# Attention rows to columns by DMA transposes, casting loads of v, and loads ordered a tile sooner, in an attention and gated-MLP kernel

## The chip, the cores and the metric

One core of one Trainium2 chip. The metric is the device time of one execution in microseconds, the slowest core's; here there is one core. Every ratio below is the mean time of one kernel's fast runs over the mean time of the other's fast runs in the same rounds, with a 95% interval, so it is not quite the ratio of the medians that stand beside it.

## The reference

```python
# q, k, v: 8 batches x 8 heads x 576 positions x 64, float32
scores = q @ k.T / 8                      # heads 0-3: window of the last 32 positions
attn   = softmax(where(mask, scores, -1e9))   # heads 4-7: every 4th of the last 128 positions
x      = (attn @ v).transpose(0, 2, 1, 3).reshape(4608, 512)
h      = x @ w_in                         # 512 -> 2048
out    = (h * sigmoid(beta * h)) @ w_out  # 2048 -> 512, float32
```

The scores are small (q and k are 0.1 times a normal draw), so the softmax is nearly flat inside its window.

## The kernel before

Everything is bfloat16 on TensorE. The 4608 tokens are cut into 9 tiles of 512. For each tile, 16 slots of w_in (four matmuls of 512 columns each, then tanh on ScalarE and a gate on VectorE) and 4 output blocks of w_out (16 matmuls each) run. Between them, in the same stream, the attention of a later batch is computed: scores S, exponentials, a multiplication by a mask, value matmuls V, and a division by the row sums ("norm"), which gives rows. The w_in matmuls need columns (`xT`), so TensorE transposes the rows:

```python
for name in [n for n in names if n[0] == "X"]:
    ...
    def back(e, x=x, j=j, g=g, n=n, m=m):
        xp = bank(g, BF16)
        for a in range(m):                      # m = 3 (96 columns each) or 4 (72 each)
            nc.tensor.transpose(xp[:, a * n:(a + 1) * n], xs[x, j][:, a]..., ident_b[0:n, 0:n])
    ...
    xcopy[b, x, j] = plan.op([act(S // 2), dve(S // 2)], put, [xop], ...)   # PSUM -> xT
```

For batches 3 to 7, q and k are cast by GpSimd's DMA into rows in DRAM (`s`), and SyncE's DMA transposes bring them into `dk`, `dq` and `raw`; engines then spread them into `qzd`, `kz` and `qd`. v is loaded in 32 bits by SyncE and cast by GpSimd when it is spread:

```python
cs = [cast(b, z, gop[b - 2, 4] + behind, b - 2 + .01 * z) for z in range(2)]
for n, (z, h0) in enumerate(((0, 4), (1, 4), (0, 0), (1, 0))):
    ...
    ld[b]["x", z, h0] = crossbar(b, z, h0, [cs[z]] + war(*key) + extra, b - 2 + .3 + .01 * n)
ld[b]["vp"], ld[b]["vd"] = load_v(b, (gop[b - 2, 6] + ..., gop[b - 2, 6] + ...), b - 2 + .35)
```

The important thing to know about `plan.op(engines, function, deps, priority)` is what it is not. It is a list scheduler that runs while the program is built. It places each operation with estimated durations and so fixes *the order* of the instructions on every engine. On the chip each engine walks down its list and waits only where data or a buffer demands it: in after, GpSimd stood 13.4 us before a spread, and casts behind that spread in its list went out at 190.0 us; put before it in f1, they went out at 168.8.

The softmax here doesn't subtract the row's maximum and nothing guards it: scores larger than these inputs give would overflow.

Of the kernel before, what the change touches and what calls it, by code (L numbers as in the profile page):

```python
# [33 lines left out]
class Plan:  # L34
# [3 lines left out]
    CAPS = {"h": 3, "o": 2, "a": 8}  # L38
# [11 lines left out]
    def run(self, filler=None, filler_until=0.0):  # L50
# [33 lines left out]
        while n_left:  # L84
# [41 lines left out]
            if o.dma:  # L126
                dma_free = max(dma_free, s + d + 900) + o.dma
                o.end = dma_free + 1100
                lanes[e].append(o.end)
# [25 lines left out]
def kernel(  # L155
# [32 lines left out]
    ADDED = 2  # L188

# [15 lines left out]
    def copy(e, out, in_):  # L205
# [23 lines left out]
    xs = {(x, j): const([QT if x < 2 else HT, 3 if x < 2 else C, 2, D], BF16, f"xs{x}{j}")  # L229
          for x in range(4) for j in range(2)}  # L230
# [3 lines left out]
    vd_st = st[0][:].bitcast(FP32).rearrange("p (f h T d) -> p f h T d", f=2, h=4, T=C)  # L234
    vp_st = st[1][:, 0:NI * 4 * D * 2].bitcast(FP32).rearrange("p (c d) -> p c d", d=D)
# [4 lines left out]
        "p (f h T d) -> p f h T d", f=2, h=4, T=C)  # L240
    kT = [const([P, WIN + S], BF16, f"kT{x}") for x in range(2)]
# [99 lines left out]
    def load(queue, args, deps, vt, kb, rate=.4, issue=750):  # L341
        return plan.op(
            [(queue, issue)],
            lambda e: dma(queue, *args), deps, vt, dma=kb * 1024 / rate / 1000)
# [15 lines left out]
    def direct_vd(b, deps, vt):  # L360
        rows = v[b, 4:8].rearrange("h (t T) d -> t h (T d)", T=C)
        dst = vd16.rearrange("p f h T d -> p f h (T d)")
        return [load("POOL", (dst[0:80, 0], rows[0:80]), deps, vt, 320, .35),
                load("POOL", (dst[:, 1], rows[16:CT]), deps, vt, 512, .35)]

    def load_v(b, deps, vt):
        rows = v[b, 4:8].rearrange("h (t T) d -> t h (T d)", T=C)
        dst = vd_st.rearrange("p f h T d -> p f h (T d)")
        d = [load("SP", (dst[0:80, 0], rows[0:80]), deps[0], vt, 320, .35),
             load("SP", (dst[:, 1], rows[16:CT]), deps[0], vt, 512, .35)]  # L370
        p = [load("SP", (vp_st, plain_v(b, 0, 0)), deps[1], vt + .001, 768, .2, 3500)]
        return p, d
# [39 lines left out]
    xcopy = {}  # L412

    def attention(b, ld, names, vts):
# [94 lines left out]
        if b < DIRECT:  # L509
            vdeps["P"] = ld["vp"] + [(fill3, fill4)[b % 2]]  # L510
            ops = []
            for f, n in ((0, 80), (1, P)):
                def spread(e, f=f, n=n):
                    copy(e, vd[kv][0:n, f, :, :, 0:D], vd16[0:n, f])
                o = plan.op([("POOL", 1050), ("DVE", 700)], spread, [ld["vd"][f], (fill3, fill4)[b % 2]] + war(("vd", kv)), vt)
                used("vd16", o)
                ops.append(o)
            wrote(("vd", kv))
            vdeps["D"] = ops
        else:  # L520
            def spread(e):
                copy(e, vp[kv][:, :, 0:D], vp_st)
            o = plan.op([("POOL", 1480), ("DVE", 1700)], spread, ld["vp"] + war(("vp", kv)), vt)
            used(("st", 1), o)
            vdeps["P"] = [o]
            ops = []
            for f, n in ((0, 80), (1, P)):
                def spread(e, f=f, n=n):
                    copy(e, vd[kv][0:n, f, :, :, 0:D], vd_st[0:n, f])
                o = plan.op([("POOL", 1050), ("DVE", 1200)], spread, [ld["vd"][f]] + war(("vd", kv)), vt)  # L530
                used(("st", 0), o)
                ops.append(o)
            wrote(("vd", kv), ("vp", kv))
            vdeps["D"] = ops
# [112 lines left out]
        for name in [n for n in names if n[0] == "X"]:  # L647
# [66 lines left out]
    def block_cols(t, tb, vts, lo, hi, cuts):  # L714
        g = Group("o")
# [68 lines left out]
    def loads(b):  # L784
        if b < DIRECT:
            base = -.9
            for n, (z, h0) in enumerate(((0, 4), (1, 4), (0, 0), (1, 0))):
                ld[b]["qk", z, h0] = direct_qk(b, z, h0, war(("st", z)), base + .01 * n)
            wrote(("st", 0), ("st", 1))
            ld[b]["vd"] = direct_vd(b, war("vd16"), base + .05)  # L790
            wrote("vd16")
            ld[b]["vp"] = direct_vp(b, [fill4], base + .06)
        else:
            behind = [ld[b - 1]["x", z, h0] for z in range(2) for h0 in (0, 4)] if b > DIRECT else []
            cs = [cast(b, z, gop[b - 2, 4] + behind, b - 2 + .01 * z) for z in range(2)]
            for n, (z, h0) in enumerate(((0, 4), (1, 4), (0, 0), (1, 0))):
                key = (("dk", b % 2, 0), ("dk", b % 2, 1)) if (z, h0) == (0, 4) else ("dq",) if h0 else (("raw", z),)
                extra = war("vd16") if not h0 else []
                ld[b]["x", z, h0] = crossbar(b, z, h0, [cs[z]] + war(*key) + extra, b - 2 + .3 + .01 * n)
                wrote(*key)  # L800
            ld[b]["vp"], ld[b]["vd"] = load_v(b, (gop[b - 2, 6] + war(("st", 0)), gop[b - 2, 6] + war(("st", 1))), b - 2 + .35)
            wrote(("st", 0), ("st", 1))
# [59 lines left out]
```

## Time and profile before

| | before |
|---|---|
| median of 3 runs | 327.26 us (327.01 to 327.35) |
| span of the profiled run | 325.7 us |
| TensorE busy | 310.3 us, 95% |
| granted TensorE clock | 0.988 |
| TensorE: sum of all matmuls at columns/2.4 + 2.5 ns | 300.6 us |
| TensorE: time between starts beyond that sum | 20.0 us, of it 16.8 before 70 us |

The last two rows are worked out from the trace: the start of each weight load against the start of the one before it, less the pitch of the matmul between them. The pitch is a fit to this trace, in which neighbouring matmuls from 120 to 300 us start 216 ns apart at 512 columns, 42 at 96, 32 at 72 and 29 at 65, in the median. "Wait" below means this excess. It adds up: 1.1 us to the first matmul, 300.6, 20.0, and 4.0 for the last output to leave, 325.7.

Two further views of before: the first is TensorE's line and the clock's in the page's 40 slices (8.1 us each, in tenths); the second is from the list of DMA issues (what, issuing queue, count, KB, median us from issue to landing).

```profile
PE   5878999999999999999999999999999999999995
PEclk9699999999999999999999999999999999999999
```

```profile
st<-in_v_dram SPq DMA_DIRECT2D x5, 768.0 KB, 8.6
...
raw<-s SPq DMA_TRANSPOSE x10, 4.0
...
dk<-s SPq DMA_TRANSPOSE x5, 9.8
dq<-s SPq DMA_TRANSPOSE x5, 4.1
```

Slices are counted from 0: a 9 from slice 4 on is a stream without a hole. v and the transposes of q and k share SyncE's queue, and dk, the first behind v, pays for it: its issue alone holds SyncE for 5.8 to 7.9 us, that of dq for 1.2 to 1.5.

### The profile page before, as it was taken

The page shows a single profiled execution, that of the slowest core. Times are in us where ns is not written, and L with a number is a line of the kernel's source. Part 1 is how long each engine was busy: PE and PEld are TensorE (multiplying, and loading weights), DVE is VectorE, ACT ScalarE, POOL GpSimd, SP SyncE. Part 2 cuts the span into 40 slices and gives each one's busy share as a digit, 9 for nine tenths or more (in the row PEclk, how much of TensorE's full clock was granted, in tenths as well). Part 3 has the DMA queues.
Part 4 walks back from the last instruction along what each step waited for, and adds up shares of the span by engine and source line. Part 5 has one row for each costly group of instructions (what it writes and reads, how often), then busy time and mean ns, then how long its engine had stood idle before and what let it go on. Part 6 is the DMA issues. An engine that isn't in the chain of part 4 may idle for free.

```text
span 325.7 us, 6483 instructions
## 1 busy us (share of the span) xinstructions
PE 310.3 (95%) x2433; PEld 176.2 (54%) x2473; DVE 222.9 (68%) x508; ACT 189.1 (58%) x364; POOL 114.6 (35%) x150
## 2 busy tenths in 40 slices
PE   5878999999999999999999999999999999999995
PEld 3766777655555545555555455545554444444453
DVE  5578777688888879887889868976885443344300
ACT  3577778577757646565746574657464544445411
POOL 7999742602863448335505520551000000000000
PEclk9699999999999999999999999999999999999999
DMA  6999999769805892699689558940000010000121
GB/s 88 173 209 208 204 163 179 142 157 223 146 0 114 235 189 86 129 225 178 166 207 178 135 112 199 190 126 32 34 32 34 32 64 33 34 32 32 45 86 64
DMA packets 69759, 40.04 MB, mean 123 GB/s; under 512 B 50832, under 2 KB 64416, under 8 KB 69408
## 3 DMA queue, kind: packets, MB, share of 16 engines
q0 software_dynamic: 20784, 16.09, 34.8%
q1 hardware_dynamic: 48800, 23.48, 31.2%
q8 instruction: 19, 0.31, 0.4%
q14 instruction: 12, 0.10, 0.1%
q10 hardware_dynamic: 144, 0.07, 0.1%
HBM read 40.37 MB, written 15.34 MB: 171 GB/s over the span
## 4 chain that ended last, share of the span: by engine, by line
PE 85%; DVE 6%; ACT 3%; issue 2%; DMA 2%; POOL 0%; ACTq 0%; DVEq 0%; POOLq 0%
PE bank L720 36%; PE bank L688 35%; PE bank L629 4%; PE bank L656 3%; PE bank L558 2%; DMA st<-in_q_dram 2%; PE bank L398 2%; PE bank L569 2%; DVE g L700 2%; DVE xs L642 2%; ACT tnh L695 1%; PE bank L552 1%; DVE qzd L206 1%; DVE kz L206 1%; PE bank L563 1%
## 5 line engine op out<-in xcount | busy, mean ns | idle before, releaser
L695 ACT ACTIVATE tnh<-bank,beta_half 128x512 bf16<-128x512 f32 (+2 forms) x160 | 102.6, 645 | 89.9 <-PE bank L688 81.5
L688 PE MATMUL bank<-xT,w_in_bf 128*128 128x512 bf16 (+2 forms) x622 | 144.6, 357 | 2.3 <-ACT pt L596 0.5
L720 PE MATMUL bank<-w_out_bf,g 128*128 128x512 bf16 (+1 forms) x570 | 142.0, 373 | 1.3 <-ACT osb L737 0.3
L700 DVE SCALAR_TENSOR_TENSOR g<-tnh,bank 128x512 bf16<-128x512 bf16 (+2 forms) x160 | 100.2, 631 | 59.4 <-ACT tnh L695 57.9
L688 PEld LDWEIGHTS <-w_in_bf 128*128 128x128 bf16 x640 | 58.3, 97 | 49.3 <-issue 3.2
L720 PEld LDWEIGHTS <-g 128*128 128x128 bf16 x592 | 53.8, 98 | 49.8 <-issue 0.5
L596 ACT ACTIVATE pt<-bank 128x288 bf16<-128x288 f32 (+1 forms) x112 | 45.1, 446 | 4.6 <-PE bank L558 2.1
L642 DVE TENSOR_TENSOR xs<-bank,rcp 72x256 bf16<-72x256 f32 (+1 forms) x96 | 44.6, 465 | 3.3
L609 POOL TENSOR_TENSOR pt<-pt,mask_d 128x288 bf16<-128x288 bf16 x22 | 17.3, 800 | 64.8 <-ACT pt L596 62.0
L629 PEld LDWEIGHTS <-pt 128*128 128x128 bf16 x448 | 22.8, 97 | 12.9 <-issue 0.6
L737 ACT ACTIVATE osb<-bank 128x512 f32<-128x512 f32 (+1 forms) x33 | 19.4, 587 | 17.8 <-PE bank L720 16.7
L656 PEld LDWEIGHTS <-xs 72*128 72x128 bf16 (+1 forms) x224 | 15.1, 97 | 13.1 <-DVE xs L642 1.7
L656 PE MATMUL bank<-ident_b,xs 72*128 72x72 bf16 (+1 forms) x224 | 18.6, 200 | 1.4 <-DVE xs L642 1.1
L206 ACT COPY xT<-bank 128x288 bf16<-128x288 bf16 x34 | 13.4, 398 | 9.9 <-PE bank L656 8.6
L206 DVE COPY xT<-bank 128x288 bf16<-128x288 bf16 x30 | 13.1, 436 | 8.0 <-PE bank L656 7.6
L641 DVE RECIPROCAL rcp<-bank 72x4 f32<-72x4 f32 (+1 forms) x96 | 16.7, 174 | 1.7 <-PE bank L629 1.5
L558 PE MATMUL bank<-qzd,dk 128*128 128x144 bf16 x128 | 17.6, 234 | 0.2
L629 PE MATMUL bank<-vd,pt 128*128 128x65 bf16 x256 | 16.5, 193 | 0.5 <-DVE xs L642 0.3
L558 PEld LDWEIGHTS <-dk 128*128 128x128 bf16 x128 | 11.4, 102 | 6.5 <-issue 0.8
L206 POOL CAST vd<-st 80x1024 bf16<-80x1024 f32 (+1 forms) x10 | 10.4, 1053 | 8.2 <-DMA st<-in_v_dram 8.2
L739 DVE TENSOR_SCALAR osb<-bank 128x512 f32<-128x512 f32 (+2 forms) x5 | 2.8, 552 | 13.7 <-PE bank L720 11.6
L609 DVE TENSOR_TENSOR pt<-pt,mask_d 128x288 bf16<-128x288 bf16 x26 | 10.2, 419 | 1.3 <-ACT pt L596 1.2
(107 smaller groups left out, 236.6 us busy)
## 6 DMA issues: line engine op xcount, KB each, us to landing
out_dram<-osb SPq DMA_DIRECT2D x35, 256.0 KB, 2.0
st<-in_v_dram SPq DMA_DIRECT2D x5, 768.0 KB, 8.6
s<-in_k_dram POOLq DMA_DIRECT2D x5, 576.0 KB, 5.7
s<-in_q_dram POOLq DMA_DIRECT2D x5, 576.0 KB, 8.4
st<-in_v_dram SPq DMA_DIRECT2D x5, 512.0 KB, 5.0
w_out_bf<-in_moe_w_out_dram POOLq DMA_DIRECT2D x2, 1024.0 KB, 21.8
st<-in_k_dram POOLq DMA_DIRECT2D x6, 288.0 KB, 9.0
st<-in_q_dram POOLq DMA_DIRECT2D x6, 288.0 KB, 10.2
```

The costliest lines, as they stand in the source:

```text
L206: (nc.scalar.copy if e == "ACT" else E[e].tensor_copy)(out=out, in_=in_)
L558: nc.tensor.matmul(sc[:, a, 0:2 * n], lhsT=dk[kv][:, rp, h4, hf * (CT - P):hf * (CT - P) + P], rhs=qzd[kv][:, :, rp, h4, hf * HT:(hf + 1) ...
L596: nc.scalar.activation(out=pt_of(x, j, n).rearrange("p (a b) n -> p a b n", a=2), in_=sc[:, :, 0:2 * n].rearrange("p a (b n) -> p a b n", ...
L609: E[e].tensor_tensor(out=w, in0=w, in1=m, op=ALU.mult)
L629: nc.tensor.matmul(pv[:, a, h2, :], lhsT=pt[x][:, c], rhs=rhs, start=True, stop=True)
L642: nc.vector.tensor_tensor(out=xs[x, jx][:, a0:a0 + m], in0=pv[0:n, :, :, 0:D], in1=rc[0:n, 0:m].unsqueeze(3).to_broadcast([n, m, 2, D]), o ...
L656: nc.tensor.transpose(xp[:, a * n:(a + 1) * n], xs[x, j][:, a].rearrange("p h d -> p (h d)"), ident_b[0:n, 0:n])
L688: nc.tensor.matmul(bank(g)[:, 0:n], lhsT=w_in_bf[:, kt, fb * P:(fb + 1) * P], rhs=xT[:, kt, xo:xo + n], start=(kt == 0), stop=(kt == NKT - 1))
L695: nc.scalar.activation(out=th[:, 0:n], in_=bank(g)[:, 0:n], func=ACT.Tanh, scale=beta_half[:, fb:fb + 1])
L700: nc.vector.scalar_tensor_tensor(out=g_t[t % 2][:, fb, c0:c0 + n], in0=th[:, 0:n], scalar=1.0, in1=bank(g)[:, 0:n], op0=ALU.add, op1=ALU.mult)
L720: nc.tensor.matmul(bank(g)[:, lo:hi], lhsT=g_t[t % 2][:, fb, tb * P:(tb + 1) * P], rhs=w_out_bf[:, fb, lo:hi], start=(fb == 0), stop=(fb = ...
L737: nc.scalar.mul(out=ob[:, cols], in_=bank(g)[:, cols], mul=0.5)
```

## The change

The intent: take 140 of the 224 transposes of rows off TensorE, which sets the end, and give DMA and the two queues more time by ordering the loads a tile sooner. Cut to its core:

```diff
-    CAPS = {"h": 3, "o": 2, "a": 8}
+    CAPS = {"h": 3, "o": 2, "z": 4, "a": 8}
...
-        g = Group("o")
+        g = Group("z" if t == NTT - 1 else "o")          # last tile: four banks
...
+    def back_dma(b, j, vt_of, vdone):                    # batches 3 to 7
+        rows = dram_pool.tile([S // 2, HD], BF16, name=f"x{b}_{j}")
+        # ... two stores of the plain heads' rows, one of the dilated heads' rows ...
+        cols = xT[:, :, b * S + j * S // 2:b * S + (j + 1) * S // 2]
+        o = plan.op([("SP", 1300)], lambda e: nc.sync.dma_start_transpose(out=cols, in_=rows[:]),
+                    out + [dil], ..., dma=1500, lat=2000)
...
-            ld[b]["vp"], ld[b]["vd"] = load_v(b, (gop[b - 2, 6] + ..., gop[b - 2, 6] + ...), b - 2 + .35)
+            ld[b]["vd"] = direct_vd(b, gop[b - 2, 0] + war(*key), b - 2 + .35)     # GpSimd's DMA, casting
+            ld[b]["vp"] = direct_vp(b, gop[b - 2, 0] + war(("vp", b % 2)), b - 2 + .36)
...
-            cs = [cast(b, z, gop[b - 2, 4] + behind, b - 2 + .01 * z) for z in range(2)]
+            cs = [cast(b, z, gop[b - 3, 12] + behind, b - 2.3 + .01 * z) for z in range(2)]
...
-                ld[b]["x", z, h0] = crossbar(b, z, h0, [cs[z]] + war(*key) + extra, b - 2 + .3 + .01 * n)
+                ld[b]["x", z, h0] = crossbar(b, z, h0, [cs[z]] + war(*key) + extra, b - 2 + .01 * n)
```

More of the change, by code (lines that the diff above doesn't have):

```diff
@@ L127, in run @@
                 dma_free = max(dma_free, s + d + 900) + o.dma
-                o.end = dma_free + 1100
+                o.end = dma_free + (o.lat or 1100)
                 lanes[e].append(o.end)
@@ L188 @@
     ADDED = 2
+    BY_DMA = 3
     pool = lambda name, bufs: ctx.enter_context(tc.tile_pool(name=name, bufs=bufs))
@@ L228 @@
     pt = [const([P, NG[x], P], BF16, f"pt{x}") for x in range(4)]
-    xs = {(x, j): const([QT if x < 2 else HT, 3 if x < 2 else C, 2, D], BF16, f"xs{x}{j}")
-          for x in range(4) for j in range(2)}
+    xsp = [const([QT, 3, 2, 2, D], BF16, f"xsp{j}") for j in range(2)]
+    xsd = [const([HT, C, 2, 2, D], BF16, f"xsd{j}") for j in range(2)]
+    xs = {(x, j): (xsp if x < 2 else xsd)[j][:, :, x % 2] for x in range(4) for j in range(2)}
     st = [const([P, 8 * 512], BF16, f"st{i}") for i in range(2)]
     ks, qs = (s[0:RT].rearrange("p (h e) -> p h e", h=H) for s in st)
-    vd_st = st[0][:].bitcast(FP32).rearrange("p (f h T d) -> p f h T d", f=2, h=4, T=C)
-    vp_st = st[1][:, 0:NI * 4 * D * 2].bitcast(FP32).rearrange("p (c d) -> p c d", d=D)
     rl = xT[0:RT, :, 6 * S:6 * S + R * P].rearrange(
@@ L240 @@
         "p (f h T d) -> p f h T d", f=2, h=4, T=C)
+    vd16_of = [vd16] * DIRECT + [st[b % 2][:, 0:2048].rearrange(
+        "p (f h T d) -> p f h T d", f=2, h=4, T=C) for b in range(DIRECT, B)]
     kT = [const([P, WIN + S], BF16, f"kT{x}") for x in range(2)]
@@ L361, in direct_vd @@
         rows = v[b, 4:8].rearrange("h (t T) d -> t h (T d)", T=C)
-        dst = vd16.rearrange("p f h T d -> p f h (T d)")
+        dst = vd16_of[b].rearrange("p f h T d -> p f h (T d)")
         return [load("POOL", (dst[0:80, 0], rows[0:80]), deps, vt, 320, .35),
                 load("POOL", (dst[:, 1], rows[16:CT]), deps, vt, 512, .35)]
-    def load_v(b, deps, vt):
-        rows = v[b, 4:8].rearrange("h (t T) d -> t h (T d)", T=C)
-        dst = vd_st.rearrange("p f h T d -> p f h (T d)")
-        d = [load("SP", (dst[0:80, 0], rows[0:80]), deps[0], vt, 320, .35),
-             load("SP", (dst[:, 1], rows[16:CT]), deps[0], vt, 512, .35)]
-        p = [load("SP", (vp_st, plain_v(b, 0, 0)), deps[1], vt + .001, 768, .2, 3500)]
-        return p, d
     scratch = {}
@@ L412 @@
     xcopy = {}
+    def back_dma(b, j, vt_of, vdone):
+        rows = dram_pool.tile([S // 2, HD], BF16, name=f"x{b}_{j}")
+        plain = rows[:, 0:HD // 2].rearrange("(i m e) c -> e m i c", e=2, m=QT // 2)
+        out = []
+        for e_ in range(2):
+            out.append(plan.op(
+                [("SP", 500)], lambda e, e_=e_: nc.sync.dma_start(
+                    out=plain[e_], in_=xsp[j][e_ * QT // 2:(e_ + 1) * QT // 2].rearrange("p a x h d -> p a (x h d)")),
+                [vdone[0, j], vdone[1, j]], vt_of[f"X1{j}"], dma=600, lat=2000))
+        dil = plan.op(
+            [("SP", 500)], lambda e: nc.sync.dma_start(
+                out=rows[:, HD // 2:].rearrange("(t r) c -> t r c", r=C),
+                in_=xsd[j][:].rearrange("p r x h d -> p r (x h d)")),
+            [vdone[x, jj] for x in (2, 3) for jj in (2 * j, 2 * j + 1)], vt_of[f"X3{j}"], dma=1100, lat=2000)
+        for x in range(4):
+            wrote(("xs", x, j))
+            for o in out if x < 2 else [dil]:
+                used(("xs", x, j), o)
+        cols = xT[:, :, b * S + j * S // 2:b * S + (j + 1) * S // 2]
+        o = plan.op([("SP", 1300)], lambda e: nc.sync.dma_start_transpose(out=cols, in_=rows[:]), out + [dil],
+                    max(vt_of[f"X1{j}"], vt_of[f"X3{j}"]), dma=1500, lat=2000)
+        for x in range(4):
+            xcopy[b, x, j] = o
     def attention(b, ld, names, vts):
@@ L508, in attention, with spread @@
         vt = vt_of["zVAL"]
-        if b < DIRECT:
-            vdeps["P"] = ld["vp"] + [(fill3, fill4)[b % 2]]
-            ops = []
-            for f, n in ((0, 80), (1, P)):
-                def spread(e, f=f, n=n):
-                    copy(e, vd[kv][0:n, f, :, :, 0:D], vd16[0:n, f])
-                o = plan.op([("POOL", 1050), ("DVE", 700)], spread, [ld["vd"][f], (fill3, fill4)[b % 2]] + war(("vd", kv)), vt)
-                used("vd16", o)
-                ops.append(o)
-            wrote(("vd", kv))
-            vdeps["D"] = ops
-        else:
-            def spread(e):
-                copy(e, vp[kv][:, :, 0:D], vp_st)
-            o = plan.op([("POOL", 1480), ("DVE", 1700)], spread, ld["vp"] + war(("vp", kv)), vt)
-            used(("st", 1), o)
-            vdeps["P"] = [o]
-            ops = []
-            for f, n in ((0, 80), (1, P)):
-                def spread(e, f=f, n=n):
-                    copy(e, vd[kv][0:n, f, :, :, 0:D], vd_st[0:n, f])
-                o = plan.op([("POOL", 1050), ("DVE", 1200)], spread, [ld["vd"][f]] + war(("vd", kv)), vt)
-                used(("st", 0), o)
-                ops.append(o)
-            wrote(("vd", kv), ("vp", kv))
-            vdeps["D"] = ops
+        vdeps["P"] = ld["vp"] + [(fill3, fill4)[kv]]
+        ops = []
+        for f, n in ((0, 80), (1, P)):
+            def spread(e, f=f, n=n):
+                copy(e, vd[kv][0:n, f, :, :, 0:D], vd16_of[b][0:n, f])
+            o = plan.op([("POOL", 1050), ("DVE", 700)], spread,
+                        [ld["vd"][f], (fill3, fill4)[kv]] + war(("vd", kv)), vt)
+            used("vd16" if b < DIRECT else ("st", kv), o)
+            ops.append(o)
+        wrote(("vd", kv))
+        vdeps["D"] = ops
         def pt_of(x, j, n):
@@ L646, in attention @@
                                   [vop] + war(("xs", x, jx)), vt - .003, group=g)
-        for name in [n for n in names if n[0] == "X"]:
+        if b >= BY_DMA:
+            for j in range(2):
+                back_dma(b, j, vt_of, vdone)
+        for name in [n for n in names if n[0] == "X" and b < BY_DMA]:
             x, j = int(name[1]), int(name[2])
@@ L798, in loads @@
                 extra = war("vd16") if not h0 else []
-                ld[b]["x", z, h0] = crossbar(b, z, h0, [cs[z]] + war(*key) + extra, b - 2 + .3 + .01 * n)
+                ld[b]["x", z, h0] = crossbar(b, z, h0, [cs[z]] + war(*key) + extra, b - 2 + .01 * n)
                 wrote(*key)
-            ld[b]["vp"], ld[b]["vd"] = load_v(b, (gop[b - 2, 6] + war(("st", 0)), gop[b - 2, 6] + war(("st", 1))), b - 2 + .35)
-            wrote(("st", 0), ("st", 1))
+            key = [("st", z) for z in range(2)] if b < DIRECT + 2 else [("st", b % 2)]
+            ld[b]["vd"] = direct_vd(b, gop[b - 2, 0] + war(*key), b - 2 + .35)
+            wrote(("st", b % 2))
+            ld[b]["vp"] = direct_vp(b, gop[b - 2, 0] + war(("vp", b % 2)), b - 2 + .36)
+            wrote(("vp", b % 2))
     def xready(lo, hi):
```

## The prediction

> **What bounds the kernel now.** I read the page's busy line first, then the chain that ended last, then the idle column of the matmul rows, and last the timeline of TensorE in the middle of the run.
>
> ```profile
> PE 310.3 (95%) x2433; PEld 176.2 (54%) x2473; DVE 222.9 (68%) x508; ACT 189.1 (58%) x364; POOL 114.6 (35%) x150
> ...
> PE 85%; DVE 6%; ACT 3%; issue 2%; DMA 2%; POOL 0%; ACTq 0%; DVEq 0%; POOLq 0%
> ```
>
> Both lines name TensorE: busy for 95% of the span, and 85% of the chain that ended last. No other engine is near full. The cost table, and the stretches 160 to 200 us and 260 to 300 us, say the same:
>
> ```profile
> L688 PE MATMUL bank<-xT,w_in_bf 128*128 128x512 bf16 (+2 forms) x622 | 144.6, 357 | 2.3 <-ACT pt L596 0.5
> L656 PE MATMUL bank<-ident_b,xs 72*128 72x72 bf16 (+1 forms) x224 | 18.6, 200 | 1.4 <-DVE xs L642 1.1
> ```
>
> ```profile
> 160.00:200.00 40.00, 39.68 (x318) 21.45 (x322) 32.71 (x77) 24.39 (x46) 11.10 (x12) 1.00 0.76 163
> 260.00:300.00 40.00, 39.84 (x184) 18.14 (x186) 15.81 (x23) 18.85 (x29) 0.00 (x0) 1.00 0.11 40
> ```
>
> The last number of a row of the cost table is the idle time just before that group: 2.3 and 1.4 us in a whole run. In the second fence the columns are length, then busy time of PE, PEld, DVE, ACT and POOL, the granted clock, the DMA share and GB/s. TensorE has 0.3 us of idle in 40, at full clock.
>
> The row L656 is the work that the change takes away: 224 transposes of the normalised rows, 18.6 us. The tempting sum is 140 of 224 times 18.6, or 11.6 us. The timeline shows why that is wrong:
>
> ```profile
> 165.20 1.03 PE L688 MATMUL bank<-xT,w_in_bf 128*128 128x512 bf16 x4
> 166.06 0.29 PE L656 MATMUL bank<-ident_b,xs 72*128 72x72 bf16 x4
> 166.19 0.29 PE L629 MATMUL bank<-vd,pt 128*128 128x65 bf16 x4
> 166.31 1.03 PE L720 MATMUL bank<-w_out_bf,g 128*128 128x512 bf16 x4
> ```
>
> Read the start column and not the duration. Four transposes of 72 columns start at 166.06, the next group at 166.19: they hold the array for 0.13 us, while the row says 0.29[...]. Four 512-column matmuls hold it for 0.86 us (165.20 to 166.06), not 1.03. That gives columns/2.4 ns plus 2.5 ns for each: 215.8 ns at 512, 32.5 at 72, 42.5 at 96.
>
> With this pitch I summed all 2473 matmuls of the program in their order: 300.6 us. The start of each weight load in the trace, set against that sum, shows where more than the pitch passes: some 14.8 us before 40 us (loads landing, the low clock, the first batch's chain), 2.2 us from 40 to 80, 1.9 us from 80 to 110, then nothing beyond tenths until 306, and 0.5 us in the tail. After 110 us the kernel is a solid stream of matmuls: a matmul taken out there is worth its pitch, and a wait put in there is paid in full if no slack covers it.
>
> [...]
>
> From the DMA view of 134 to 140 us, while the casts of a k and q pair ran:
>
> ```profile
> q0 software_dynamic: 74, 1.07, 98.8%
> q1 hardware_dynamic: 101, 0.11, 6.1%
> ```
>
> The columns are packets, MB and the share of the engines' time. The cast's packets are 18 KB each, the hardware queue's at most 2 KB. [...] A DMA transpose that falls into a cast will crawl.
>
> **The change part by part.**
> 1. *Transposes off TensorE.* Batches 3 to 7 lose 8 bursts each: four of 4 x 32.5 ns and four of 3 x 42.5 ns, 1.03 us. Five batches: 5.15 us. The built program's sum falls from 300.6 to 295.4 us, the same. All of it lies in the solid part. Gain 5.15 us.
> 2. *Evacuations off ACT and DVE.* 40 copies into xT go (8 a batch, 398 ns on ACT or 436 on DVE), some 16 us over two engines at 58% and 68%. Neither bounds, so this is worth only waits: the two of 0.5 us near 81 and 106 us may change. I count 0.5 us.
> 3. *Last tile's outputs in four banks.* The last half block waited for a bank: the trace has TensorE idle 0.30 us before 320.07, my sum 0.46. Gain 0.4 us.
> 4. *All casts by DMA.* POOL loses five vp casts of 1.47 us and gets cheaper vd copies; at 35% busy this is worth nothing. The v loads leave the hardware queue. There they held the dk transposes back: issue to landing took 9.8 us for dk against 4.1 for dq, although both move the same bytes. The new transposes should then take about 4 us.
> 5. *New DMA work.* Each batch stores and transposes 0.59 MB, at an estimated 200 GB/s of the measured streams some 6 us of DMA a batch in a period of 32 us. It fits.
> 6. *The new chain to xT.* Norm 0.65 us (reciprocal and multiply), store about 3, issue 1.3, transpose about 4, so 9 us, where a TensorE transpose and a copy took 1. I placed every matmul of the new program by the pitch: between the last value matmul that a column tile needs and the first w_in matmul that reads it lie 19.9, 24.1, 19.1, 20.1 and 18.1 us of other matmuls for tiles 3 to 7, and over 30 for tile 8. So the chain is hidden unless SP, in order, holds a transpose up.
>
> That can happen. In SP's order the second transpose of batch 3 stands behind two transposes for batch 5, which wait for a cast issued just when the first w_in slots of tile 2 are done. I estimate its landing at 112 to 114 us on the scale of summed pitch, with the need at 115.0. The first transpose of batch 5 stands behind an output store, issues at about 157.5 and lands at about 162, needed at 164.7; the last casts start at about 160. Batch 6's first: 194.5 against 197. These three have 1 to 3 us of slack, so I charge 1 us in the mean.
> 7. *Tile 3's order.* Its w_in slots are put off and run in groups of three to six without output matmuls between, on three banks. A slot's bank is held for 0.86 us of matmuls, 0.69 of tanh, 0.69 of gate and hand-overs, some 2.6 us, so three banks give one slot per 0.88 us against 0.86, and ACT and DVE have other work too. I charge 0.7 us.
> 8. *Loads a tile sooner.* The software queue is full from 4 to 58 us, and batch 3's casts (8 us for the pair, from their landings) now stand before batch 2's q and k. The new order needs batch 2's k 6.3 us of matmul later than the old one, where it had some 6 us of slack: about 4 us are left. I charge 0.4 us.
>
> Sum: 327.3 - 5.15 - 0.5 - 0.4 + 1.0 + 0.7 + 0.4 = 323.3 with all the charges. Each charge is as likely to be zero as not, so I lean to the lower side and say 322.4.
>
> **The rivals.**
> - *A late transpose becomes the bound.* For it: [...]SP is in order. Against: 18 us and more of other matmuls in front of each reader. If a chain misses at every tile by 3 us, five tiles give 15 us, and the time is 335 or more.
> - *The busy time was right.* If the transposes had cost 83 ns each, the gain would be 11.6 us and the time near 315. Against: the starts in the timeline.
> - *DMA becomes the bound.* The casts move at 150 to 200 GB/s and the hardware queue shares the engines; batch 2 late by 5 us in the early part would cost up to 5 us once, giving 327.
> - *All hidden.* 327.3 - 6.05 = 321.2, and without the early and middle waits of 1.9 us from 80 to 110, near 320.
>
> **Range and chances.** The floor is about 320, since there is little else to remove. One missed landing of 3 us brings 325. So 320.2 to 325.4. Faster by over 2% means below 320.7, which needs every charge to be zero: 0.2. Slower by over 2% needs a miss at every tile: 0.04. The rest is within 2%: 0.76.
>
> **What would show it.** Right: 84 matmuls left in the xs transpose group; 0.86 us steps after 120 us; no idle of TensorE put down to a DMA into xT; from issue to landing about 4 us for the new transposes. Wrong: w_in matmuls that wait for the scratch rows in DRAM above 1 us, at tiles 3, 5 or 6; TensorE idle before 100 us grown by over 2 us with q or k loads of batch 2 named; a drop in total much nearer 11 us than 5.

The rival's 83 ns are the 18.6 us of the row L656 over its 224 transposes. That a transpose will crawl beside a cast was the estimate from the DMA view alone (0.11 MB beside 1.07); g3 below measures it. The store of "about 3" us in step 6 was an estimate whose source is not given; the output stores of before landed in 2.0 us in the median, the stores of the plain heads' rows in after in 3.7.

## More of the kernel before

The dependence `gop[b - 2, 4]` ("the gate of slot 4 of tile b - 2") is there for the order alone: no semaphore on the chip stands for it.

```python
o = plan.op([("DVE", 900), ("POOL", 1150)], spread, [ld["x", 1, 4], ...])         # dq  -> qzd
o = plan.op([("POOL", 1200), ("DVE", 1400)], spread, [ld["x", 0, 0], ...])        # raw -> kz
sdone[x, j] = plan.op([("POOL", 120 + 2.2 * 4 * n), ("DVE", 160 + .65 * 4 * n)], mask, ...)
```

GpSimd (POOL) thus has four kinds of work in one list: DMA issues, spreads, masks and constants.

## The result, and the profile after

| | before | after |
|---|---|---|
| median (4 runs each, same rounds) | 327.19 us (327.01 to 327.35) | 348.38 us (347.51 to 350.57) |
| ratio of fast runs | | 1.0658 (1.0608 to 1.0708) |
| span of the profiled run | 325.7 us | 345.8 us |
| sum of matmuls at their pitch | 300.6 us | 295.4 us |
| wait of TensorE beyond it | 20.0 us | 45.5 us |

The change is 6.6% slower; the prediction said 322.4 us. The two last rows close the account: 25.5 us more wait, 5.15 us less work, 20.3 us against 20.1 between the spans. The gain that was promised on TensorE came to the last tenth, and five times as much was lost.

The page of after, the lines that answer to those of before:

```profile
PE 312.2 (90%) x2333; PEld 171.0 (49%) x2333; DVE 215.4 (62%) x485; ACT 183.8 (53%) x348; POOL 125.5 (36%) x159
...
PE   5889999989998499999997909979999999999995
...
PEclk9899999999999699999999978999999999999999
...
PE 67%; DVE 11%; DMA 7%; issue 5%; ACT 5%; POOL 4%; SPq 0%; ACTq 0%; POOLq 0%; DVEq 0%
...
L695 PE MATMUL bank<-xT,w_in_bf 128*128 128x512 bf16 (+2 forms) x640 | 146.4, 361 | 10.8 <-DMA xT<-x 8.7
```

Three things are to be read here. PE has holes now: slices 8 (69 to 78 us; the slices are 8.6 us here), 12 and 13 (104 to 121), 21 (182 to 190), 23 (199 to 207, a 0) and 26 (225 to 233). The clock dips at the two deepest holes, to six tenths in slice 13 and seven in slice 23. And the chain has "DMA" and "DVE" where it had TensorE; the w_in row has 8.7 us of idle that one DMA into xT ended.

Where the wait of TensorE lies, in us by stretch of each kernel's own run (the other columns are experiments told below):

| stretch, us | before | after | f1 | e8 | e7 | f4 |
|---|---|---|---|---|---|---|
| 0 to 70 | 16.8 | 16.0 | 16.1 | 19.2 | 16.2 | 16.4 |
| 70 to 90 | 1.2 | 4.4 (D) | 4.4 | 4.6 | 1.0 | 1.2 |
| 90 to 110 | 0.8 | 0.5 | 0.5 | 0.0 | 0.1 | 0.3 |
| 110 to 130 | 0.3 | 7.8 (A) | 8.3 | 1.0 | 0.0 | 0.0 |
| 130 to 160 | 0.3 | 1.0 | 0.9 | 0.4 | 0.7 | 0.1 |
| 160 to 200 | -0.1 | 2.8 (B) | 2.7 | 0.5 | 3.4 | 0.6 |
| 200 to 220 | 0.1 | 10.1 (C) | 0.1 | 1.6 | 0.0 | 0.3 |
| 220 to 240 | 0.0 | 2.6 (B) | 2.6 | 0.0 | 1.2 | 0.3 |
| 240 to the end | 0.6 | 0.3 | 0.2 | 0.1 | 0.1 | 0.1 |
| sum | 20.0 | 45.5 | 35.8 | 27.4 | 22.9 | 19.3 |

**Hole C, 207 us.** TensorE's timeline, then SyncE's, then GpSimd's (start us, duration us, then what; in brackets the idle time before and what ended it):

```profile
198.29 0.28 PE L562 MATMUL bank<-qzd,dk 128*128 128x144 bf16 x2
207.32 1.89 PE L695 MATMUL bank<-xT,w_in_bf 128*128 128x512 bf16 x4 [8.74 <-DMA xT<-x]
```

```profile
191.66 8.07 SPq L428 DMA_TRANSPOSE xT<-x  x1
199.82 1.00 SPq L415 DMA_DIRECT2D x<-xsp  x2
```

```profile
182.10 3.15 POOL L207 COPY kz<-raw 64x1152 bf16<-64x1152 bf16 x2 [13.38 <-PE bank L573]
185.30 2.36 POOL L207 COPY qzd<-dq 64x1152 bf16<-64x1152 bf16 x2
187.72 2.33 POOL L207 COPY qd<-raw 64x1152 bf16<-64x1152 bf16 x2
190.00 0.53 POOL L341 DMA_DIRECT2D s<-in_k_dram  x1
190.52 0.53 POOL L341 DMA_DIRECT2D s<-in_q_dram  x1
191.04 1.43 POOL L341 DMA_DIRECT2D st<-in_v_dram  x2
```

Read from below. GpSimd was idle for 13.4 us, because its next entry, a spread of batch 6 into `kz`, had to wait for the last score of batch 5, which reads `kz`. Only behind three such pairs stand the casts of batch 7. They go out at 190.0 us, and 1.7 us later SyncE issues the transpose of the first rows of batch 5, which tile 5 needs. Its issue alone takes 8.1 us (1.3 us at best in this run), it lands 15.6 us after its start, and TensorE waits. The first four matmuls after the hole take 1.89 us and not 1.03: the granted clock is 0.50 from 207.3 to 209 us (1.00 from 212 to 216), and the first seven starts are 0.40 to 0.43 us apart at 512 columns, as against 0.216 in the stream.

The chain of waits of the same stretch names nothing else:

```profile
190.46 0.61 ACT osb L744
...
191.66 15.62 DMA xT<-x
...
207.32 2.74 PE bank L695 x6
```

From the DMA view of after, 192 to 198 us, then 198 to 207 us (queue: packets, MB, share of the engines' time):

```profile
q0 software_dynamic: 64, 0.88, 83.6%
q1 hardware_dynamic: 47, 0.03, 1.9%
```

```profile
q0 software_dynamic: 2621, 0.65, 84.2%
q1 hardware_dynamic: 1812, 0.80, 61.2%
```

In the first six microseconds, beside the casts, the hardware queue moved 0.03 MB. None of it was the transpose: the trace has 43 packets of 512 bytes and 4 of 2 KB there, which are the rows of the two stores that SyncE had issued just before (at 190.05 and 191.09 us). A transpose of x moves in 1152 packets of 256 bytes (so in e7 at 247 us, where nothing else runs), and the first of these starts at 199.1 us, 7.5 us after the issue and not 1.3 as in e7. So the casts held up SyncE's whole queue, with the transpose at its end (g3 and e5b below: its first packet came 7.1 us after the issue beside the casts alone, 1.4 with neither casts nor loads). From 198 us on the casting loads of v ran beside it, with packets of 250 bytes in the mean, and it took 8.2 us from its first packet to its landing.

**Hole A, 117 us.** GpSimd's timeline, then TensorE's:

```profile
98.28 1.49 POOL L341 DMA_DIRECT2D st<-in_v_dram  x2
99.76 1.44 POOL L341 DMA_DIRECT2D vp<-in_v_dram  x1
111.92 2.34 POOL L207 COPY qzd<-dq 64x1152 bf16<-64x1152 bf16 x2 [10.73 <-DMA dq<-s]
114.33 2.02 POOL L207 COPY vd<-st 80x1024 bf16<-80x1024 bf16 x2
116.32 1.41 POOL L613 TENSOR_TENSOR pt<-pt,mask_d 128x288 bf16<-128x288 bf16 x2
```

```profile
117.10 0.40 PE L633 MATMUL bank<-vd,pt 128*128 128x65 bf16 x4 [5.80 <-POOL pt L613]
```

Two masks of batch 3 stand in GpSimd's list behind spreads of batch 4, and the first of those waits 10.7 us for the transpose of `dq`. That transpose was issued at 101.0 us, right behind GpSimd's own casting loads of v (98.3 to 101.2 us). TensorE waits for the mask, not for anything of batch 4. That the order of the list matters here is read from these lines; no run moved the masks.

**Holes B, 187 and 231 us.** VectorE's timeline at the first:

```profile
182.12 1.78 DVE L613 TENSOR_TENSOR pt<-pt,mask_d 128x288 bf16<-128x288 bf16 x2
183.83 2.82 DVE L613 TENSOR_TENSOR pt<-pt,maske_PP 128x384 bf16<-128x384 bf16 x2
```

Four masks take 4.6 us. In this run a mask of 288 columns takes 0.31 us in the median and 1.56 at most. The slow ones run exactly while GpSimd makes its spreads (from 182.10 us, above). Experiment e6 tests this.

**D, 70 to 90 us.** Two waits of 0.97 and 0.63 us before the scores of batch 2 and a number of smaller ones: the casts of batch 3 now stand before the loads of batch 2 on the software queue. The wait follows these casts: 4.6 us in e8, where they are as soon and v is with SyncE, and 1.2 in e3, where they are late.

The landings, from the list of DMA issues of after. The list's medians rest on the landings that the trace could assign: 6 of the 10 for xT, 4 of 5 for dk, only 2 of 5 for dq (4.4 and 11.7 us; the dq of hole A, which its reader puts at 10.9, isn't among them). The new transposes have the median that was foretold, with two late ones (9.0 and 15.6 us). dk gained 2.7 us.

```profile
raw<-s SPq DMA_TRANSPOSE x10, 4.6
xT<-x SPq DMA_TRANSPOSE x10, 4.2
...
dk<-s SPq DMA_TRANSPOSE x5, 7.1
dq<-s SPq DMA_TRANSPOSE x5, 8.1
```

### The profile page after: what moved, and what is told of

Read it like the earlier page. It is cut to its first block, busy times and chain, and to the rows that moved or that the text cites. A ratio compares the mean times of both kernels' runs of the same rounds, so it can differ in the third digit from the quotient of the medians.

```text
span 345.8 us, 6210 instructions
## 1 busy us (share of the span) xinstructions
PE 312.2 (90%) x2333; PEld 171.0 (49%) x2333; DVE 215.4 (62%) x485; ACT 183.8 (53%) x348; POOL 125.5 (36%) x159
## 4 chain that ended last, share of the span: by engine, by line
PE 67%; DVE 11%; DMA 7%; issue 5%; ACT 5%; POOL 4%; SPq 0%; ACTq 0%; POOLq 0%; DVEq 0%
PE bank L727 30%; PE bank L695 29%; DMA xT<-x 5%; DVE pt L613 4%; PE bank L633 3%; DMA st<-in_q_dram 3%; DVE g L707 2%; ACT tnh L702 2%; DVE xsd L646 2%; PE bank L562 1%; POOL pt L613 1%; POOL st L341 1%; PE bank L573 1%; PE bank L556 1%; DVE rcp L645 1%
## 5 line engine op out<-in xcount | busy, mean ns | idle before, releaser
L727 PE MATMUL bank<-w_out_bf,g 128*128 128x512 bf16 (+1 forms) x592 | 145.4, 375 | 0.0
L633 PEld LDWEIGHTS <-pt 128*128 128x128 bf16 x448 | 22.9, 98 | 26.3 <-issue 7.4
L744 ACT ACTIVATE osb<-bank 128x512 f32<-128x512 f32 (+2 forms) x35 | 20.3, 586 | 18.7 <-PE bank L727 15.6
L646 DVE TENSOR_TENSOR xsd<-bank,rcp 72x256 bf16<-72x256 f32 x64 | 26.9, 421 | 2.2
L207 POOL COPY kz<-raw 64x1152 bf16<-64x1152 bf16 x10 | 15.1, 1512 | 34.1 <-DMA out_dram<-osb 19.9
L633 PE MATMUL bank<-vd,pt 128*128 128x65 bf16 x256 | 16.8, 196 | 11.1 <-POOL pt L613 5.8
L645 DVE RECIPROCAL rcp<-bank 72x4 f32<-72x4 f32 (+1 forms) x96 | 16.8, 175 | 8.8 <-PE bank L633 8.6
L646 DVE TENSOR_TENSOR xsp<-bank,rcp 96x384 bf16<-96x384 f32 x32 | 17.7, 554 | 1.1
L613 POOL TENSOR_TENSOR pt<-pt,mask_d 128x288 bf16<-128x288 bf16 x15 | 11.1, 761 | 18.5 <-ACT pt L600 18.3
L207 POOL COPY vd<-st 80x1024 bf16<-80x1024 bf16 (+1 forms) x10 | 10.6, 1067 | 19.6 <-DMA st<-in_v_dram 19.6
L341 POOL DMA_DIRECT2D vp<-in_v_dram x9 | 12.0, 1330 | 7.2 <-PE bank L633 5.8
L207 POOL COPY qzd<-dq 64x1152 bf16<-64x1152 bf16 x9 | 10.5, 1163 | 11.1 <-DMA dq<-s 10.7
L613 DVE TENSOR_TENSOR pt<-pt,maske_PP 128x384 bf16<-128x384 bf16 x18 | 12.4, 703 | 0.4 <-ACT pt L600 0.3
## 6 DMA issues: line engine op xcount, KB each, us to landing
st<-in_q_dram POOLq DMA_DIRECT2D x6, 288.0 KB, 16.2
```

The costliest lines, as they stand in the source:

```text
L207: (nc.scalar.copy if e == "ACT" else E[e].tensor_copy)(out=out, in_=in_)
L613: E[e].tensor_tensor(out=w, in0=w, in1=m, op=ALU.mult)
L633: nc.tensor.matmul(pv[:, a, h2, :], lhsT=pt[x][:, c], rhs=rhs, start=True, stop=True)
L645: nc.vector.reciprocal(out=rc[0:n, 0:m], in_=pv[0:n, :, :, D])
L646: nc.vector.tensor_tensor(out=xs[x, jx][:, a0:a0 + m], in0=pv[0:n, :, :, 0:D], in1=rc[0:n, 0:m].unsqueeze(3).to_broadcast([n, m, 2, D]), o ...
L727: nc.tensor.matmul(bank(g)[:, lo:hi], lhsT=g_t[t % 2][:, fb, tb * P:(tb + 1) * P], rhs=w_out_bf[:, fb, lo:hi], start=(fb == 0), stop=(fb = ...
```

## The experiments

Three theories stood at the outset: the new transposes by DMA are what TensorE waits for, because of their long chain; the sooner order of the loads costs; the casting loads of v on the second queue cost. Before measured 327.4 to 327.5 us in each group of runs.

**e1: the change with all transposes on TensorE.**

```diff
-    BY_DMA = 3
+    BY_DMA = 8
```

> The changed kernel with the transposes of all batches back on TensorE; casts by DMA, earlier loads and the four banks kept. Theory 1 (DMA transposes crawl when the software queue is busy: the 9 us stall at tile 5 is the x transpose beside the casts of batch 7, the 6.2 us stall at 117 us is the dq transpose beside the v loads of batch 4): the first stall goes, the second stays, the transposes cost 5 us again: 338 to 344 us. Theory 2 (the chain store-then-transpose into xT is the whole cause): about 327 us. Theory 3 (the earlier loads and the order they bring are the whole cause): 348 us or more.

Measured: 347.3 us (345.8 to 349.0), ratio 1.061. Taking the transposes by DMA out again gives back 1.1 us of 21, which the spread of the runs hardly separates; the time lies in none of the three ranges, 0.7 us below the third. TensorE waits 5.2 us at 120 us and 1.9 to 2.3 us at 160, 195 and 230; the wait for xT is gone, but other waits take its place. The transposes are not the cause by themselves.

**e2: before with the transposes by DMA alone.** The `back_dma` of the change and `BY_DMA = 3` in the kernel before, nothing else.

> The kernel before with only the stores and DMA transposes of batches 3 to 7 added; loads, v casts and banks as before. Theory 1: the casts of the kernel before are issued early in a tile, the x transposes late in one, so they meet less: 321 to 329 us. Theory 2 (the chain itself is the cause): 335 us or more, with waits of w_in matmuls for xT of several us. Theory 3: about 322 us.

Measured: 325.9 us (325.5 to 327.4), ratio 0.997 (0.993 to 1.000). No w_in matmul waits for a transpose of x: the ten are issued in 1.3 to 1.6 us each, and the one landing that the trace has took 3.3 us. The long chain is hidden there. Of the 5.15 us, 1.5 arrive (spans 325.7 and 324.2): TensorE has 3.3 us of new wait, most of it at 173 to 178 us before V matmuls.

**e3: the change with the loads as late as before.**

```diff
-  cast(b, z, gop[b - 3, 12] + behind, b - 2.3 + ...)        direct_vd(b, gop[b - 2, 0] + ...)
+  cast(b, z, gop[b - 2, 4] + behind, b - 2 + ...)           direct_vd(b, gop[b - 2, 6] + ...)
```

(and the transposes of q and k at + .3, `direct_vp` like `direct_vd`)

> The changed kernel with the casts, k and q transposes and v loads planned as late as in the kernel before; DMA transposes and v casts by DMA kept. Theory 1: the casts fall elsewhere and no longer run beside the x transpose of tile 5, but the v loads stay on the software queue: 325 to 338 us, the largest wait for xT under 4 us. Theory 2: 343 us or more, since the chain is the same. Theory 3: about 322 us.

Measured: 332.0 us (330.8 to 332.7), ratio 1.014. D is back at before's 1.2 us and A is gone; a w_in matmul waits 3.5 us at 157 us for a transpose of x that took 7.9 us. So the order matters much. Against e7 below, which has v with SyncE, TensorE waits 7.3 us more: that wait of 3.5 us, 2.2 us before V matmuls at 180 to 183 us, and the rest in small pieces.

**e4: the change without the casts of batch 7** (its transposes read the rows of batch 5; the other engines' orders are the same).

> The changed kernel with the two casts of batch 7 left out and the scratch of batch 5 read in their place (a wrong result for batch 7, on purpose); the order of all other instructions is the same. Theory 1: the x transpose issued near 191 us lands in 4 to 6 us and not 15.6, and the 9 us wait at tile 5 goes: 338 to 340 us. Theory 2 (the transpose is late because SP is in order behind an output store, or the chain is long): no change, 347 to 350 us.

Measured: 342.1 us (339.9 to 343.5), ratio 1.045. The wait at C falls from 9.0 to 4.3 us, the landing from 15.6 to 11.0. Both lie between the two theories: the casts are a part of C, and so is something else.

**e5b: the change without the loads of v for batches 4 and 7 and the casts of batch 7.**

```diff
+            if b in (4, 7):  # no load: an empty operation in the plan
+    vd16_of[4] = vd16_of[3]
```

> The changed kernel without the casting loads of v for batches 4 and 7 and without the casts of batch 7 (wrong result on purpose; the work of TensorE, VectorE and ScalarE is in the same order, and the spreads read values of an earlier batch). Theory 1, the software queue's casting loads slow the DMA transposes that run beside them: the transpose of dq for batch 4 lands in under 6 us in place of 10.9, and the 5.8 us wait of the V matmuls of batch 4 at about 111 us shrinks by 3 us or more; the last transpose of x before tile 5 lands in 3 to 5 us in place of 15.6 and the 9 us wait at 207 us is under 1 us. Time 331 to 337 us. Theory 2, the transposes come late because GpSimd and SyncE reach them late in their own order: the wait at 111 us stays within 1 us of 5.8 and the one at 207 us is still over 3 us, time 341 to 345 us.

Measured: 331.2 us, one run. (The expectation calls the waiting V matmuls those of batch 4; by the name of their buffer they are batch 3's.) GpSimd's timeline:

```profile
94.92 3.23 POOL L621 TENSOR_TENSOR pt<-pt,mask_d 128x288 bf16<-128x288 bf16 x4
105.06 2.34 POOL L207 COPY qzd<-dq 64x1152 bf16<-64x1152 bf16 x2 [6.91 <-DMA dq<-s]
```

dq was issued at 101.1 us and its spread starts at 105.06: some 3.9 us, and not 10.9. The stretch 110 to 130 us falls from 7.8 to 1.5 us of wait, and C is gone: the transpose lands in 3.9 us, and from 182 to 214 us TensorE waits 0.2 us in all. Theory 1 of that run holds at both places: the transposes are slow because loads run beside them on the other queue.

**e6: the change without GpSimd's spreads of batches 6 and 7.**

```diff
+                    if not (b >= 6 and e == "POOL"):
                         copy(e, dst, raw[rows, 0])          # and the same for qzd and qd
```

> The changed kernel with GpSimd's copies into qzd, kz and qd left out for batches 6 and 7 (wrong result on purpose; TensorE, VectorE and ScalarE keep their order). Theory 1, GpSimd's copies hold VectorE's multiplication by a mask back: the longest multiplication by a mask after 180 us takes under 0.5 us in place of 1.6, and the two waits of 2.7 us on TensorE at about 187 and 231 us are under 0.7 us each; time 342.5 to 345. Theory 2, the masks only come late because their exponentials do: the multiplications still take up to 1.5 us and the waits stay, time 347 to 349.

Measured: 333.7 us, one run, almost 9 us below the expected range. B is as theory 1 has it: both waits vanish (0.2 us in 180 to 190 and 0.1 in 220 to 240 us), and the four masks at the same place in VectorE's list take 1.2 us:

```profile
183.36 0.52 DVE L616 TENSOR_TENSOR pt<-pt,mask_d 128x288 bf16<-128x288 bf16 x2
183.80 0.68 DVE L616 TENSOR_TENSOR pt<-pt,maske_PP 128x384 bf16<-128x384 bf16 x2
```

A mask of 288 columns took 0.30 us alone and up to 1.56 beside spreads. By what mechanism a spread holds it up, no run shows.

The miss taught more than the hit. C vanished as well, though neither casts nor loads had been taken out. Without the spreads in front of them, GpSimd issued the casts at 169.2 us and not at 190.0, and the transpose of x, issued at 190.3, met only one load of v and landed in 6.7 us or less. That gave the next test.

**f1: the same loads, moved on GpSimd alone.** Nothing is left out: the casts and the two vd loads of batch 7 are issued right before the spreads of batch 6. TensorE, VectorE, ScalarE and SyncE have the same lists to the last instruction.

```diff
                 copy(e, vd[kv][0:n, f, :, :, 0:D], vd16_of[b][0:n, f])
+                if (b, f) == (6, 1):
+                    for issue in early:        # casts and vd loads of batch 7
+                        issue("POOL")
```

> The changed kernel with one thing moved: GpSimd issues the casts and the two casting vd loads of batch 7 right before its copies into kz, qzd and qd of batch 6, which wait for the last scores of batch 5, and not right after them. Nothing is left out and all other engines keep their order. Theory 1, the 9 us wait at 207 us exists because those copies hold the casts back until 1.7 us before the last transpose of x for tile 5: the casts go out at about 169 us, that transpose lands in under 8 us, the wait is under 1 us, the time is 337 to 340 us. Theory 2, any place of these loads costs the same: the wait turns up elsewhere, 345 us or more.

Measured: 337.9 us (2 runs), ratio 1.032, as theory 1 has it. GpSimd and SyncE:

```profile
168.84 0.53 POOL L341 DMA_DIRECT2D s<-in_k_dram  x1
...
182.58 3.12 POOL L207 COPY kz<-raw 64x1152 bf16<-64x1152 bf16 x2 [11.26 <-PE bank L582]
```

```profile
192.11 1.94 SPq L434 DMA_TRANSPOSE xT<-x  x1
```

The issue takes 1.9 us and not 8.1, and the stretch 200 to 220 us has 0.1 us of wait and not 10.1. Hole C, half of the loss, is four DMA issues that stood behind the wrong wait in one engine's list.

**f5: does the size of the casts' packets matter?** The casts of batch 7 in 288 rows of 2 KB and not 32 of 18 KB.

```diff
-  dst.rearrange("x (a e) -> (x a) e", e=1024)
+  dst.rearrange("x (a e) -> a x e", e=1024)
```

> The changed kernel, but the casts of batch 7 write the same bytes in rows of 2 KB, 288 of them, in place of 32 rows of 18 KB. Same bytes, same queue, same time of issue. Theory 1, the transpose of x starves because the casts' packets are eighteen times its own[...]: it lands in 12 us or less in place of 15.6 and the wait at 207 us falls from 9 to 5.5 us or less. Theory 2, the bytes in flight alone slow it: 15 us and 8 to 10 us as in the changed kernel.

Measured: 349.1 us (2 runs), not separable from the change's 348.4. The transpose lands in 12.7 us and the wait is 6.1, between the theories and just outside the first one's range. (Its "eighteen times its own" is wrong: the transpose's packets are 256 bytes, the stores' before it 512 and 2048.) With smaller packets of the casts the transpose's first packet goes after 5.7 us and not 7.5, and it lands 3 us sooner. The whole gains nothing: the stretch 220 to 240 us has 4.2 us of wait and not 2.6, which was not followed up.

**g3: casts of batch 7 kept, its loads of v left out**, the counterpart of e4.

> The changed kernel without the three casting loads of v of batch 7, its casts of q and k kept where they are (wrong result on purpose, all other engines in the same order). With neither of them the wait at 207 us was gone, with the loads of v alone it was 4.3 us and the transpose of x landed in 11.0 us, with both 9.0 and 15.6. If the casts' share is what is left, 4 to 5 us of wait and a landing in 10 to 12 us; if the loads of v behind the casts are what carries the transpose past the start of the tile, under 2 us and under 9.

Measured: 342.9 us, one run; landing in 9.9 us, wait 3.2 us. It too fell between its two ranges. With neither the wait is 0, with the casts alone 3.2, with the loads of v alone 4.3, with both 9.0, so 1.4 us come only with both. ("Neither" is e5b, which also leaves out the loads of v for batch 4.) The packets say what each does. With the casts alone the transpose's first packet starts 7.1 us after the issue and it lands 2.8 us later; with the loads of v alone it starts after 3.5 us and lands 7.5 us later; with neither, 1.4 and 2.5. The casts mostly delay the start, the loads of v mostly stretch the transfer.

**e7 and e8: which of the two moves of the loads costs?** e7 is e2 with the four banks of the last tile. e8 is e7 with casts and transposes of q and k ordered as soon as in the change, while v stays with SyncE in 32 bits:

```diff
-  cast(b, z, gop[b - 2, 4] + behind, b - 2 + ...)     crossbar(..., b - 2 + .3 + .01 * n)
+  cast(b, z, gop[b - 3, 12] + behind, b - 2.3 + ...)  crossbar(..., b - 2 + .01 * n)
```

> The kernel before with the DMA transposes and with four banks for the last tile's output; loads and casts as before. If the four banks are worth what the last half block's wait was, 0.4 us less than the DMA transposes alone (325.9 us): 325.2 to 325.8. If the banks take room from others, 326 to 327.

Measured: 325.45 us (325.2 to 325.8), ratio 0.993 (0.989 to 0.997): 0.45 us less than e2, which lies inside e2's spread (325.5 to 327.4); what shows the banks' worth is the trace, where the wait of 0.46 us before the last half block is gone.

> The last one with the casts and the transposes of q and k ordered as soon as in the changed kernel, but v still loaded in 32 bits by SyncE on the hardware queue, and spread by GpSimd. Theory 1, the casting loads of v on the software queue are what costs: within 1 per cent of the kernel before, 325 to 330 us. Theory 2, the sooner order by itself costs (the casts of q and k fall beside the transposes of x): 336 us or more, with a wait of several us of a w_in matmul for a transpose of x.

Measured: 327.0 us (326.1 to 329.7), ratio 0.997 (0.991 to 1.002): theory 1. From its list of DMA issues (medians of 3 landings of xT and of one of dq):

```profile
xT<-x SPq DMA_TRANSPOSE x10, 3.7
...
dq<-s SPq DMA_TRANSPOSE x5, 4.0
```

With e3 and the change this makes a square, all four with transposes by DMA and four banks (median us):

| | v in 32 bits by SyncE | v cast by GpSimd's DMA |
|---|---|---|
| order of the loads as before | 325.45 (e7) | 332.0 (e3) |
| ordered sooner | 327.0 (e8) | 348.4 (the change) |

(In the lower right the loads of v are sooner too; in the lower left only casts and transposes.) Sooner alone costs 1.5 us, v by casting DMA alone 6.6, both 22.9, far more than the sum. These are prices of whole plans: in all four the scheduler gave every engine another order, so the square doesn't separate a collision on the DMA engines from a worse order elsewhere. What does is f1, where one place in one list is worth 10.5 of the 22.9 us, and e5b.

**f4 and e9: versions that should beat both.** f4 is e7 with the spreads into `kz` and `qzd` offered to ScalarE first; e9 is e7 with the planned landing of stores and transposes of x cut from 2 us to 0.7 to 0.9.

```diff
-  plan.op([("POOL", 1200), ("DVE", 1400)], spread, [ld["x", 0, 0], ...])   # kz
+  plan.op([("ACT", 1140), ("POOL", 1500)], spread, [ld["x", 0, 0], ...])
-  plan.op([("DVE", 900), ("POOL", 1150)], spread, [ld["x", 1, 4], ...])    # qzd
+  plan.op([("ACT", 1140), ("DVE", 1150)], spread, [ld["x", 1, 4], ...])
```

> The kernel before with the DMA transposes and four banks (325.45 us), where the copies into kz and half of those into qzd of batches 3 to 7 may go to ScalarE in place of GpSimd. Theory 1, most of the 4 us that TensorE still waits there at 130 to 140, 170 to 180 and 220 to 240 us are masks that VectorE does slowly beside GpSimd's copies: 322.5 to 324.5 us. Theory 2, ScalarE's exponentials come later and give it back: 325 to 328.

Measured: 322.26 us (321.95 to 322.37), ratio 0.984 (0.981 to 0.987), just under theory 1's range and the best of all. The wait in 160 to 200 us falls from 3.4 to 0.6 us and that in 220 to 240 from 1.2 to 0.3: with 295.4 us of matmuls and 19.3 us of wait the whole gain of the transposes is there. The theory behind it is not shown, and e7's trace speaks against it: no slow mask of VectorE there runs beside a copy into `kz` or `qzd`. They run beside GpSimd's own masks (5.5 us over the usual time of a mask, summed over the run) and its casts of v (1.0), and f4 still has 5.4 us of such excess. Moving the spreads also changed the order of many other instructions; the hit owes something to luck, and the cause of the gain stays open.

> The kernel before with the DMA transposes and four banks, where the plan counts 0.7 to 0.9 us in place of 2 us for the landing of each store and transpose of x, so that the next tile is ordered sooner. No wait of TensorE there is for xT, so I expect no gain: 325 to 326 us; over 327 if a w_in matmul now waits for a transpose.

Measured: 323.4 us (322.5 to 326.2), ratio 0.990 (0.984 to 0.996). I expected no gain and was wrong: a new order happened to take most of the wait at 170 to 180 us away (2.9 to 0.7 us). Why that order is better was not settled.

**g1: f4 and e9 together.**

> The copies by ScalarE (322.26 us) and the shorter planned landing (323.39 against 325.45 us) together. Each took away mostly the same waits of TensorE near 170 to 180 us, so little is left to gain: 321 to 322.5 us.

Measured: 324.4 us (323.5 to 327.0), ratio 0.992. A miss: the two do not add, there are 1.8 us of new wait at 160 to 170 us. f4 stays the version to keep.

## Why the prediction was wrong, point by point

- *Transposes off TensorE, 5.15 us (step 1)*: right. The sum of pitches fell by 5.15 us, and f4 collected it all. The busy time would have promised 11.6 us.
- *Evacuations, 0.5 us (step 2)*: right; of the two waits of 0.5 us near 81 and 106 us, the second is gone in e2.
- *Four banks, 0.4 us (step 3)*: right; the wait of 0.46 us is gone in e7.
- *Casts of v by DMA, worth nothing (step 4)*: the step that failed first. "The v loads leave the hardware queue" was read as "they leave the transposes alone". They share the same DMA engines, only from another queue: the profile books both queues on the same 16 (192 to 198 us of after: 83.6% of their time for the software queue, 1.9% for the hardware queue). On SyncE's queue v stood in SyncE's own order, ahead of dk, which had time, and no w_in matmul of e7 waited for a transpose of x (the one landing that its trace has took 3.5 us); on GpSimd's it runs beside whatever SyncE has in flight. The dq of hole A took 10.9 us, and 3.9 in e5b without the loads of v beside it; the late transpose of x took 15.6, and 9.9 in g3 without them. e3 against e7 puts the price of the two plans at 6.6 us with nothing ordered sooner.
- *The chain to xT, 1 us (step 6)*: the right transpose was named, the first of batch 5 (on the scale of summed pitch; 41.5 us of waits lie between that scale and the trace at 207 us). But it was placed 2.5 us ahead of the last casts, "issues at about 157.5" and "the last casts start at about 160", and so was given a landing of 4 to 5 us. On the chip the casts came 1.7 us *ahead* of it, and 9.0 us of wait followed, 10.1 with the slow restart. The same text had said that a transpose that falls into a cast will crawl (as it did: 9.9 us beside the casts alone in g3, 3.9 in e5b with neither casts nor loads). Two planned times 2.5 us apart on two engines without a semaphore between them are not an order. The rival "a late transpose becomes the bound" was the right mechanism, at one tile and not at all five. The prediction's own sign of being wrong, a w_in matmul that waits over 1 us for the scratch rows at tile 5, came.
- *Tile 3's order, 0.7 us (step 7)*: the number came by luck. There is a wait of 0.74 us at 145.8 us, but before the first w_in matmul of tile 3, so no group of slots had used up its banks. A norm of VectorE ended it, and that stood behind two masks which took 2.5 us and not 0.7 beside GpSimd's spread into `kz`, as in B:

```profile
142.71 2.52 DVE L613 TENSOR_TENSOR pt<-pt,maske_PP 128x384 bf16<-128x384 bf16 x2
145.83 1.89 PE L695 MATMUL bank<-xT,w_in_bf 128*128 128x512 bf16 x8 [0.58 <-DVE xsd L646]
```

- *Loads a tile sooner, 0.4 us (step 8)*: right mechanism, wrong size: 3.2 us (4.4 against 1.2 in 70 to 90 us).
- *What no step had*: GpSimd's list. It was weighed by its busy share ("at 35% busy this is worth nothing"). A (7.5 us, from 0.3 to 7.8) is masks that stand in it behind spreads which wait for a DMA. B (2.9 and 2.6 us) is VectorE's masks held up by its spreads; e6 shows it. A share of 36% says nothing about what waits behind the head of an in-order list (10.7 us at A, 13.4 before the casts of C).

The sum of terms in place of the foretold ones: A 7.5, B 5.5, C 10.0, D 3.2, the stretch with tile 3's start 0.7, less 0.3 in the tail, less 1.1 before 70 and from 90 to 110 us, 25.5 in all; less 5.15 of matmuls, 20.3 us.

## What to carry to other kernels

Moving loads from one DMA queue to another does not take them off the engines: it takes them out of the one order in which urgent transfers could stand first (here a transpose landed in 15.6 us beside casts and loads on the other queue, and in 3.9 without them), so before moving them, list which transfer with a reader close by will be in flight at the same time. In an engine that works its list in order, look for the entry that waits and at what stands behind it, not at the busy share: four DMA issues moved ahead of such an entry were worth 10 us here. A scheduler's dependence that no semaphore stands for fixes an order on one engine and nothing between two, so events planned a few us apart have to be taken in both orders when the time is estimated.
